# Loading and casting v three pairs later, and issuing the last weight pieces later, in a fused attention and MLP kernel

## The chip, the cores and the metric

The kernel runs on one core of one Trainium2 chip. The metric is the device time of one execution in microseconds (us); lower is better. Engines are named as in the profile: PE is TensorE (matmul), PEld its weight load, DVE is VectorE, ACT is ScalarE, POOL is GpSimd, SP is SyncE, which here issues most of the DMA transfers.

## The reference

There are 8 batches, 12 heads, 448 positions and a head dimension of 64. The inputs are float32, and so is the output.

```python
scores = scale * np.matmul(q, k.transpose(0, 1, 3, 2))
m = np.max(scores, axis=-1, keepdims=True)
e = np.exp(scores - m)
attn = e / (np.sum(e, axis=-1, keepdims=True) + np.exp(-m) + 1e-09)
x = np.matmul(attn, v)              # then (B, H, S, D) -> (3584, 768)

h = x @ w_in                        # 768 x 2048
sp = np.where(h > 20.0, h, np.log1p(np.exp(np.minimum(h, 20.0))))
out = (h * np.tanh(sp)) @ w_out     # 2048 x 768
```

## The kernel before, in words

**Pairs and units.** The work on attention is cut into 48 pairs of heads (6 pairs to a batch). Pairs 0 to 5 form the head of the program, a loop over `p` with four steps `s` each. From pair 6 on, three pairs make a unit `u` (unit 2 is pairs 6 to 8, the third set of three pairs; unit 15 is pairs 45 to 47; units 16 to 19 have no attention left). The loop of a unit has twelve steps `n`, four to each pair.

**One pair.** `load_pair` issues the transfers of q, k and v (224 KB each) on SP into buffers of which there are three for each name. `cast_pair` and `cast_v` turn them into bf16 on POOL (lines 179, 180 and 186). `transpose_pair` (line 206) turns q and k on PE, and `evac_qk` copies them out of PSUM, q as `qd` (line 252 for the later pairs) and k as `kT` (line 260). `scores` (lines 309 to 326) makes the scores on PE and their negative row maximum on DVE (line 330); `exps` takes exponentials on ACT into `en` (line 343). `denominators` and `normalise` follow: from pair 12 on, `normalise` multiplies `en` by the reciprocal on DVE, seven instructions to a pair (line 412); for nearly all pairs a DMA transpose on SP then makes `eT` out of `en` (line 420). `av_pair` multiplies `eT` by v on PE (line 460) and copies the result into `xT`.

**The MLP.** After the twelve steps of a unit come eight groups of six matmuls `x @ w_in` (`mm1_mish`, line 496), each followed by mish on ACT (line 502). The matmuls with `w_out` (`mm2_part`, line 549) are spread over the steps of later units as filler by the table `plan`; the first that read the right half of w_out stand in unit 5.

**Order of the work.** The order on each engine is written out by hand, and each engine, SP and POOL included, works through its queue in that order. In the head, step `s == 3` of pair `p` issues the load of pair `p + 5` and then the DMA transpose of pair `p`, and step `s == 2` casts pair `p + 3`. In a unit, steps 0, 3 and 6 (`LOAD_AT`) load one pair, four ahead of the place (`LEAD`), and cast one pair, three ahead. All three transposes of a unit are issued on SP behind the unit's twelve steps; the next unit's loads are queued behind them.

**The weights.** They come in 20 pieces, in this order: 12 of w_in (256 KB each), 4 of the left half of w_out and 4 of its right half (384 KB each). `load_w` issues them from POOL's queue (line 162). The table `W_AT` says how many go out at which step of units 2, 3 and 4. Where `W_BEHIND` names a pair, POOL first copies a mark out of that pair's `eT` (line 157), so POOL waits until that transpose has landed. Two more places call `load_w` by themselves: two pieces in the head at `p == 1`, and three pieces with a mark on pair 8 behind the fourth matmul group of unit 2.

```python
W_AT = ({0: 4, 5: 1}, {1: 2, 3: 1, 5: 1, 7: 1, 9: 1}, {1: 1, 3: 1, 5: 1, 7: 1})
W_BEHIND = {(0, 0): HEAD - 2, (2, 1): HEAD + 4}
```

`HEAD` is 6. So the marks of the table are on pair 4 (unit 2, step 0) and on pair 10 (unit 4, step 1).

Of the kernel before, what the change touches and what calls it, by code (L numbers as in the profile page):

```python
# [19 lines left out]
def kernel(  # L20
# [27 lines left out]
    N_PAIRS = B * HP  # L48
# [59 lines left out]
    def flush_late():  # L108
        while late:
            late.popleft()()  # L110
# [10 lines left out]
    def load_pair(p, names="qkv"):  # L121
        if p >= N_PAIRS:
            return
        b, h0 = p // HP, (p % HP) * 2
        for nm in names:
            src = dict(q=q, k=k, v=v)[nm]
            t = ld_pool.tile([SP_, 2, NT * D], FP32, tag=f"{nm}_f", name=f"{nm}_f")
            nc.sync.dma_start(
                out=t, in_=src[b, h0 : h0 + 2].rearrange("h (p t) d -> p h (t d)", t=NT)
            )  # L130
            loaded.setdefault(p, {})[nm] = t
# [33 lines left out]
    def cast_pair(p, with_v=True):  # L165
        if p >= N_PAIRS:
            return
        q_f, k_f, v_f = (loaded[p].get(nm) for nm in "qkv")
        q_bf = bf_pool.tile([SP_, NT, 2, D], BF16, tag="q_bf", name="q_bf")
        k_bf = bf_pool.tile([SP_, NT, 2, D], BF16, tag="k_bf", name="k_bf")  # L170
        v_bf = bf_pool.tile([SP_, 2, NT * D], BF16, tag="v_bf", name="v_bf", bufs=12)
        by_t = "p h (t d) -> p t h d"
        q_t, k_t = (t.rearrange(by_t, t=NT) for t in (q_f, k_f))
        if p == 0:
            nc.vector.tensor_copy(out=k_bf, in_=k_t)
            for half in (slice(0, NT // 2), slice(NT // 2, NT)):
                nc.vector.tensor_copy(out=q_bf[:, half], in_=q_t[:, half])
        else:
            nc.gpsimd.tensor_copy(out=q_bf, in_=q_t)  # L179
            nc.gpsimd.tensor_copy(out=k_bf, in_=k_t)  # L180
        casted[p] = (q_bf, k_bf, v_bf)
        if with_v:
            cast_v(p)

    def cast_v(p):
        nc.gpsimd.tensor_copy(out=casted[p][2], in_=loaded.pop(p)["v"])  # L186

    def transpose_pair(p, bank=None):
# [93 lines left out]
    def scores_ahead(limit):  # L282

        while rg["next"] < limit and rg["used"] < len(sc_tiles):
            rg["used"] += 1
            scores(rg["next"])
            rg["next"] += 1
# [301 lines left out]
    LEAD = UNIT_PAIRS + 1  # L589
    LOAD_AT = (0, 3, 6)  # L590
    HEAD = HP
# [2 lines left out]
    AV_AT = {0: {1: 3, 5: 4, 8: 5}, 1: {1: 8, 4: 6, 8: 7}}  # L594
    RDEN_AT = {0: {0: 3, 2: 4, 6: 5}, 1: {0: 8, 2: 6, 6: 7}, 2: {3: 10, 5: 11}}

    W_AT = ({0: 4, 5: 1}, {1: 2, 3: 1, 5: 1, 7: 1, 9: 1}, {1: 1, 3: 1, 5: 1, 7: 1})
    W_BEHIND = {(0, 0): HEAD - 2, (2, 1): HEAD + 4}
    for p, names in (0, "kq"), (1, "qk"), (0, "v"), (2, "qk"), (1, "v"), (2, "v"):
        load_pair(p, names)  # L600
    keep_busy(8, bank=sc_tiles[0][:, 0, :])
    for p in range(2):
        cast_pair(p, with_v=False)
        transpose_pair(p)
        if p == 0:
            evac_qk(p)
            scores_ahead(3)
    load_pair(3)
    cast_v(0)
    cast_pair(2, with_v=False)  # L610
    cast_v(1)
    cast_v(2)
    load_pair(4)


    for p in range(HEAD):
        for s in range(STEPS):
            exps(p * STEPS + s)
            if s == 0 and p == 0:
                evac_qk(1, act=True)  # L620
            flush_late()
            if s == 1:
                late.extend(held)
                held.clear()
                flush_late()
            if s == 2:
                evac_qk(p + 2, act=p % 2 == 0)
            scores_ahead(HEAD * STEPS + 3)
            if s == 0:
                transpose_pair(p + 2)  # L630
                if p:
                    denominators(p - 1)
            if s == 1 and p:
                turn_on_pe(p - 1, NT - 1)
            if s == 3 and p == 1:
                load_w(2)
            if s == 2:
                if p >= 3:
                    spread_rden(p - 3)
                cast_pair(p + 3)  # L640
            if s == 3:
                if p >= 3:
                    av_pair(p - 3, hold=True)
                if p + 5 < 10:
                    load_pair(p + 5)
                normalise(p, dma=p not in BY_PE)
            if s < 3:
                keep_busy(2, half=p)
    denominators(HEAD - 1)

    for u in range(UNITS_PER_B, N_UNITS + 2 * UNITS_PER_B):
        attn = u < N_UNITS
        filler = deque()
        for part in plan.get(u, []):
            filler.extend(mm2_part(*part))
        total, done, acc = sum(w for _, w in filler), 0, 0.0
        p0 = u * UNIT_PAIRS
        if attn and u >= first_mm2:
            av_with.update({p0 + i: p0 + i - UNIT_PAIRS for i in range(UNIT_PAIRS)})
        end = min((u + 1) * UNIT_PAIRS, N_PAIRS) * STEPS  # L660

        for n in range(steps):
            pi, s = divmod(n, STEPS)
            p, idx = p0 + pi, p0 * STEPS + n
            late_tp = u == UNITS_PER_B and n == STEPS
            exps(idx)
            if u == UNITS_PER_B + 1 and n == 0:
                for j in range(2):
                    turn_on_pe(HEAD, j, busy_first=3)
            flush_late()  # L670
            if late_tp:
                transpose_pair(p0 + 2)
                evac_qk(p0 + 2)
            if held and n == 1:
                late.extend(held)
                held.clear()
                flush_late()
            late.extend(slow)
            slow.clear()
            acc += weight[n]  # L680
            want = int(total * acc / sum(weight) + 1e-6)
            while done < want:
                fn, w = filler.popleft()
                fn()
                done += w
            scores_ahead(end)
            if n in LOAD_AT:
                load_pair(p0 + LOAD_AT.index(n) + LEAD)
                cast_pair(p0 + LOAD_AT.index(n) + LEAD - 1)
            for pe, n0 in BY_PE.items():  # L690
                j = n - n0
                first = 2 if pe == HEAD else 0
                if pe // UNIT_PAIRS == u - 1 < first_mm2 - 1 and first <= j < NT:
                    turn_on_pe(pe, j, busy_first=1)
            spread = RDEN_AT.get(u - UNITS_PER_B, {})
            if n in spread:
                on_act = u < first_mm2
                spread_rden(
                    spread[n], copy=nc.scalar.copy if on_act else nc.vector.tensor_copy,
                    behind=slow if on_act else late,  # L700
                )
            early = AV_AT.get(u - UNITS_PER_B)
            if early is not None and n == 7:
                keep_busy(6, bank=mo_free[0])
            if early is not None:
                if n in early:
                    av_pair(early[n], half=p)
            elif s == (2 if pi else 0) and N_PAIRS <= p < N_PAIRS + UNIT_PAIRS:
                av_pair(p - UNIT_PAIRS)
            if u - UNITS_PER_B < len(W_AT):  # L710
                at = (u - UNITS_PER_B, n)
                load_w(W_AT[at[0]].get(n, 0), behind=W_BEHIND.get(at))
        assert done == total

        moe = u < N_UNITS + UNITS_PER_B
        b, w = (u - UNITS_PER_B) // UNITS_PER_B, u % UNITS_PER_B
        nxt = p0 + UNIT_PAIRS
        todo = sorted(range(p0, nxt), key=lambda p: p in BY_PE)
        for f in range(FF_U):
            if moe:  # L720
                mm1_mish(b, w * FF_U + f)
            if u == UNITS_PER_B and f == 3:
                load_w(3, behind=p0 + 2)
            if not attn:
                continue
            if f == 0:
                denominators(p0, UNIT_PAIRS)
                for p in todo if p0 < LATE_DIV else todo[:1]:
                    normalise(p, dma=p not in BY_PE)
            if f == 5 and u == UNITS_PER_B + 1:  # L730
                spread_rden(p0, copy=nc.scalar.copy)
            if f == 4:
                scores_ahead(min(nxt * STEPS + 1, N_PAIRS * STEPS))
            if f in (1, 3, 5):
                transpose_pair(nxt + f // 2, bank=f // 2 % 2)
                evac_qk(nxt + f // 2)
            if f >= FF_U - 2:
                scores_ahead(min(nxt * STEPS + f - FF_U + 4, N_PAIRS * STEPS))
            if f in (3, FF_U - 1) and p0 >= LATE_DIV:
                p = todo[1 + f // (FF_U - 1)]  # L740
                normalise(p, dma=p not in BY_PE)
# [32 lines left out]
```

## Time and profile before

| | |
|---|---|
| median of 3 runs | 483.12 us (481.99 to 483.59) |
| the profiled execution | 483.9 us, span 482.0 us |
| mean granted TensorE clock | 0.992 |
| busy share of PE, DVE, ACT, POOL | 95%, 75%, 72%, 22% |
| moved by DMA | 91.10 MB, 189 GB/s over the span |
| HBM read, written | 45.61 MB, 11.01 MB |
| POOL waiting for marks on `eT` | 27.2 us in 3 waits, the longest 13.8 us |

The profile is of one execution. The span runs from the first to the last instruction; the time of an execution has a little more around it, 1.9 us here. An engine's busy share is a mean over the whole span, in which stages with different limits follow one another. A timeline line gives the start, the length, the engine, the line of the kernel, the operation with what it writes and reads, the number of instructions merged into it, and in brackets the idle time before it and what ended that. For SP the length of a line is the time that the issue took, not the transfer; when a transfer has landed is a time of its own in the trace.

### The profile page before, as it was taken

The numbers are of one execution on the slowest core, as the hardware profiler recorded it, in microseconds if no ns is written. First come the engines' busy times: TensorE is split into PE (matmuls) and PEld (weight loads), VectorE is DVE, ScalarE is ACT, GpSimd is POOL, SyncE is SP. The second block draws the span as 40 slices with busy tenths as digits, with TensorE's granted clock in tenths as the row PEclk, the third lists the DMA queues.
The fourth block names the chain that finished last, engine by engine and source line by source line (L and its number), as shares of the span: only waits on it lengthen the run. The fifth ranks groups of instructions, "written<-read, shape, count | busy, mean of one in ns | idle before, by whom it ended". The sixth has DMA issues, their size and how long they took to land.

```text
span 482.0 us, 9366 instructions
## 1 busy us (share of the span) xinstructions
PE 460.2 (95%) x3291; PEld 257.7 (53%) x3291; DVE 360.3 (75%) x715; ACT 345.3 (72%) x907; POOL 104.3 (22%) x187
## 2 busy tenths in 40 slices
PE   7788899999899999999999999999999999999996
PEld 2344445545555555556555565555555565556563
DVE  5989748669899888889898998888898879421021
ACT  5998868888687869788797968787887978312300
POOL 4633618106022220404040311204040200000000
PEclk9989999999999999999999999999999999999999
DMA  8999999999999979998999999989979695961122
GB/s 238 228 207 220 239 204 216 160 197 248 211 251 228 250 157 211 229 182 224 201 251 164 256 164 219 220 193 227 194 222 197 160 175 121 154 141 34 34 66 67
DMA packets 204976, 91.10 MB, mean 189 GB/s; under 512 B 161792, under 2 KB 201472, under 8 KB 204928
## 3 DMA queue, kind: packets, MB, share of 16 engines
q1 hardware_dynamic: 197408, 84.18, 81.1%
q0 software_dynamic: 7488, 6.29, 9.0%
q8 instruction: 26, 0.43, 0.4%
q14 instruction: 22, 0.18, 0.1%
q10 hardware_dynamic: 32, 0.02, 0.0%
HBM read 45.61 MB, written 11.01 MB: 117 GB/s over the span
## 4 chain that ended last, share of the span: by engine, by line
PE 65%; DVE 7%; ACT 6%; DMA 6%; issue 1%; SPq 0%; DVEq 0%
PE mo L549 23%; PE mo L496 22%; PE sc L309 7%; ACT en L343 6%; PE sc L460 5%; DMA eT<-en 5%; DVE negm L330 4%; PE sc L496 3%; PE sc L206 3%; DVE en L412 1%; DVE xT L473 1%; PE mo L460 1%; DVE o_sb L532 0%; DMA out_dram<-o_sb 0%; DVE qd L252 0%
## 5 line engine op out<-in xcount | busy, mean ns | idle before, releaser
L343 ACT ACTIVATE en<-sc,negm 128x448 bf16<-128x448 f32 x336 | 209.2, 644 | 22.3 <-DVE negm L330 20.6
L330 DVE TENSOR_REDUCE negm<-sc 128x2 f32<-128x896 f32 x192 | 182.8, 970 | 40.6 <-PE sc L309 30.1
L549 PE MATMUL mo<-w_out_sb,gT 128*128 128x384 bf16 (+1 forms) x1024 | 166.7, 306 | 0.4 <-DVE rb L400 0.4
L496 PE MATMUL mo<-xT,w_in_sb 128*128 128x448 bf16 x672 | 142.2, 352 | 1.3 <-DMA w_in_sb<-in_moe_w_in_dram 0.9
L549 PEld LDWEIGHTS <-gT 128*128 128x128 bf16 x1024 | 96.3, 98 | 56.0 <-issue 1.9
L502 ACT ACTIVATE gT<-mo 128x448 bf16<-128x448 f32 x112 | 59.5, 543 | 81.1 <-PE mo L496 80.9
L496 PEld LDWEIGHTS <-w_in_sb 128*128 128x128 bf16 x768 | 72.5, 98 | 65.0 <-issue 3.2
L412 DVE TENSOR_SCALAR en<-en,rden 128x448 bf16<-128x448 bf16 x252 | 74.7, 369 | 0.8
L179 POOL CAST q_bf<-q_f 112x512 bf16<-112x512 f32 x47 | 29.2, 622 | 211.7 <-DMA q_f<-in_q_dram 191.2
L309 PE MATMUL sc<-kT,qd 128*128 128x448 bf16 x252 | 71.6, 354 | 1.8 <-DVE qd L252 1.8
L343 ACT ACTIVATION_READ_ACCUMULATOR en<-sc,negm 128x1 f32 x336 | 72.1, 215 | 0.0
L532 DVE COPY o_sb<-mo 128x384 f32<-128x384 f32 (+1 forms) x64 | 31.9, 498 | 48.3 <-PE mo L549 48.1
L460 PE MATMUL sc<-eT,v_bf 112*64 112x448 bf16 x336 | 39.8, 357 | 1.7 <-DMA eT<-en 0.9
L309 PEld LDWEIGHTS <-qd 128*128 128x128 bf16 x252 | 24.5, 98 | 30.7 <-issue 12.9
L252 DVE TENSOR_SCALAR qd<-sc 64x448 bf16<-64x448 bf16 x72 | 27.8, 386 | 6.0 <-PE sc L206 5.2
L186 POOL CAST v_bf<-v_f 112x512 bf16<-112x512 f32 x48 | 30.0, 625 | 5.7 <-DMA v_f<-in_v_dram 5.4
L180 POOL CAST k_bf<-k_f 112x512 bf16<-112x512 f32 x47 | 29.3, 624 | 7.2 <-DMA k_f<-in_k_dram 5.9
L460 PEld LDWEIGHTS <-v_bf 112*64 112x64 bf16 x384 | 19.8, 109 | 20.5 <-issue 11.8
L260 ACT COPY kT<-sc 128x448 bf16<-128x448 bf16 x39 | 20.8, 533 | 0.6 <-PE sc L206 0.6
L496 PE MATMUL sc<-xT,w_in_sb 128*128 128x448 bf16 x96 | 20.8, 352 | 0.0
L473 DVE CAST xT<-sc 128x448 bf16<-128x448 f32 x33 | 20.3, 615 | 0.0
L206 PEld LDWEIGHTS <-q_bf 112*128 112x128 bf16 x192 | 13.5, 97 | 9.2 <-issue 1.0
(61 smaller groups left out, 281.2 us busy)
## 6 DMA issues: line engine op xcount, KB each, us to landing
k_f<-in_k_dram SPq DMA_DIRECT2D x48, 224.0 KB, 5.0
q_f<-in_q_dram SPq DMA_DIRECT2D x48, 224.0 KB, 4.8
v_f<-in_v_dram SPq DMA_DIRECT2D x48, 224.0 KB, 5.2
w_in_sb<-in_moe_w_in_dram POOLq DMA_DIRECT2D x12, 256.0 KB, 9.5
w_out_sb<-in_moe_w_out_dram POOLq DMA_DIRECT2D x8, 384.0 KB, 10.4
out_dram<-o_sb SPq DMA_DIRECT2D x7, 336.0 KB, 4.0
out_dram<-o_sb SPq DMA_DIRECT2D x8, 288.0 KB, 4.6
out_dram<-o_sb SPq DMA_DIRECT2D x8, 240.0 KB, 3.2
```

Source lines behind the costliest of these rows:

```text
L179: nc.gpsimd.tensor_copy(out=q_bf, in_=q_t)
L180: nc.gpsimd.tensor_copy(out=k_bf, in_=k_t)
L186: nc.gpsimd.tensor_copy(out=casted[p][2], in_=loaded.pop(p)["v"])
L309: nc.tensor.matmul(sc[:, bk, 0:S], lhsT=qT[:, i].rearrange("d h r -> d (h r)"), rhs=kT, start=True, stop=True,)
L330: half_max[p] = nc.vector.tensor_reduce(out=negm, in_=sc[:, 0 : len(cols), 0:S], axis=AX.X, op=ALU.max, negate=True)
L343: e = nc.scalar.activation(out=st["en"][:, :, c, 0:SP_], in_=sc[:, bk, 0:S].rearrange("q (j c) -> q j c", j=NT), func=AF.Exp, bias=st["neg ...
L412: nc.vector.tensor_scalar(out=en[:, :, i, 0:SP_], in0=en[:, :, i, 0:SP_], scalar1=st["rden"][:, i : i + 1], scalar2=None, op0=ALU.mult,)
L460: mm = nc.tensor.matmul(av[h * 64 : (h + 1) * 64, 0:S], lhsT=v_bf[:, h, j * D : (j + 1) * D], rhs=e_h, start=(j == 0), stop=(j == NT - 1),)
L496: nc.tensor.matmul(h_ps[:, 0:S], lhsT=w_in_sb[:, dm, ff * 128 : (ff + 1) * 128], rhs=xT[b][:, dm, :], start=(dm == 0), stop=(dm == DM_T - 1),)
L502: nc.scalar.activation(out=gT[:, ff, b % 2 * S : b % 2 * S + S], in_=h_ps[:, 0:S], func=AF.Mish)
L532: nc.vector.tensor_copy(out=o_sb[:, cols.start : cols.start + n_dve], in_=st["o"][:, 0:n_dve])
L549: nc.tensor.matmul(st["o"][:, 0:n_cols], lhsT=gT[:, ff, i * 128 : (i + 1) * 128], rhs=w_out_sb[:, ff, cols], start=(ff == 0), stop=(ff == ...
```

## The change

In the head, pairs 0 to 6 are loaded with their v as before, and pairs 7, 8 and 9 without it; v of pairs 6, 7 and 8 is not cast there. In the units, steps 0, 3 and 6 still load q and k four pairs ahead and cast q and k three ahead, but the v that they load is one pair ahead and the v that they cast is the pair of the place itself. So unit 2 loads v of pairs 7, 8 and 9 and casts v of 6, 7 and 8, and the last v's are loaded and cast in unit 15.

Of the weights, the last four pieces (the right half of w_out) are issued in unit 4 at steps 3 (one), 5 (one) and 7 (two) where it was one each at steps 1, 3, 5 and 7. The casts of pair 16 stand ahead of them at step 3. The mark on pair 10 is left out.

```diff
     def cast_v(p):
+        if p >= N_PAIRS:
+            return
         nc.gpsimd.tensor_copy(out=casted[p][2], in_=loaded.pop(p)["v"])
...
-    W_AT = ({0: 4, 5: 1}, {1: 2, 3: 1, 5: 1, 7: 1, 9: 1}, {1: 1, 3: 1, 5: 1, 7: 1})
-    W_BEHIND = {(0, 0): HEAD - 2, (2, 1): HEAD + 4}
+    W_AT = ({0: 4, 5: 1}, {1: 2, 3: 1, 5: 1, 7: 1, 9: 1}, {3: 1, 5: 1, 7: 2})
+    W_BEHIND = {(0, 0): HEAD - 2}
...
             if s == 2:
                 if p >= 3:
                     spread_rden(p - 3)
-                cast_pair(p + 3)
+                cast_pair(p + 3, with_v=p + 3 < HEAD)
             if s == 3:
                 if p >= 3:
                     av_pair(p - 3, hold=True)
                 if p + 5 < 10:
-                    load_pair(p + 5)
+                    load_pair(p + 5, "qkv" if p + 5 <= HEAD else "qk")
                 normalise(p, dma=p not in BY_PE)
...
             if n in LOAD_AT:
-                load_pair(p0 + LOAD_AT.index(n) + LEAD)
-                cast_pair(p0 + LOAD_AT.index(n) + LEAD - 1)
+                at = p0 + LOAD_AT.index(n)
+                load_pair(at + LEAD, "qk")
+                load_pair(at + 1, "v")
+                cast_pair(at + LEAD - 1, with_v=False)
+                cast_v(at)
```

## The prediction

> **What bounds the kernel now.** I read the page first, then the chain of waits in order of time, then the timelines of PE, SP, POOL and DVE up to 125 us, and the trace's landing time of each transfer. The page:
>
> ```profile
> PE 460.2 (95%) x3291; PEld 257.7 (53%) x3291; DVE 360.3 (75%) x715; ACT 345.3 (72%) x907; POOL 104.3 (22%) x187
> ...
> PE 65%; DVE 7%; ACT 6%; DMA 6%; issue 1%; SPq 0%; DVEq 0%
> ```
>
> PE is busy for 460.2 of 482.0 us. Its idle time before single instructions, where it is over 0.15 us, adds up to 16.2 us, and all but 0.28 us of that lies before 122.1 us: from there on PE runs without a gap, so an edit can win only what it takes out of the first quarter (or lose what it adds anywhere). The DMA part of the chain is one transfer, and behind it stands a DVE step:
>
> ```profile
> 76.17 25.10 DMA eT<-en
> ...
> 101.31 0.95 PE sc L460 x8
> ...
> 116.31 2.93 DVE en L412 x5
> 119.23 1.48 issue
> 120.72 0.57 DVE en L412 x2
> ...
> 122.05 0.55 PE sc L309 x2
> ```
>
> A transpose has a median of 6.7 us from issue to landing (page, part 6); the one of pair 9, issued at 76.17, needed 25.10. PE's timeline gives the three late stalls that I work with:
>
> ```profile
> 58.48 1.69 PE L496 MATMUL mo<-xT,w_in_sb 128*128 128x448 bf16 x8 [0.92 <-DMA w_in_sb<-in_moe_w_in_dram]
> ...
> 101.31 0.95 PE L460 MATMUL sc<-eT,v_bf 112*64 112x448 bf16 x8 [0.86 <-DMA eT<-en]
> ...
> 122.05 0.55 PE L309 MATMUL sc<-kT,qd 128*128 128x448 bf16 x2 [1.75 <-DVE qd L252]
> ```
>
> Counted from matmul start to matmul start, the first is 1.08 us (58.485 - 57.216 - 0.189), with 0.28 us more at 64.10, on the piece that landed at 64.06; the second about 1.0 us. What comes before them is SP's queue in the head:
>
> ```profile
> 30.03 0.41 SPq L128 DMA_DIRECT2D v_f<-in_v_dram  x1
> 30.53 4.47 SPq L420 DMA_TRANSPOSE eT<-en  x1
> 35.10 0.53 SPq L128 DMA_DIRECT2D q_f<-in_q_dram  x1
> ...
> 43.02 0.41 SPq L128 DMA_DIRECT2D v_f<-in_v_dram  x1
> 43.53 3.93 SPq L420 DMA_TRANSPOSE eT<-en  x1
> 47.55 0.53 SPq L128 DMA_DIRECT2D q_f<-in_q_dram  x1
> ```
>
> SP runs back to back from 28.9 to 54.3 us. The transpose of pair 4 starts at 43.53, though ACT ended that pair's exponentials at 34.9: SP is 8.7 us late. POOL's mark on that transpose ends its wait at 50.14, right after the landing at 50.09, and only then do four w_in pieces go out:
>
> ```profile
> 50.14 0.18 POOL L157 COPY marks<-eT 1x2 bf16<-1x2 bf16 x1 [2.66 <-DMA eT<-en]
> 50.27 2.88 POOL L162 DMA_DIRECT2D w_in_sb<-in_moe_w_in_dram  x4
> ...
> 104.35 0.18 POOL L157 COPY marks<-eT 1x2 bf16<-1x2 bf16 x1 [13.78 <-DMA eT<-en]
> 104.58 0.79 POOL L162 DMA_DIRECT2D w_out_sb<-in_moe_w_out_dram  x1
> 112.49 0.61 POOL L179 CAST q_bf<-q_f 112x512 bf16<-112x512 f32 x1 [7.12 <-DMA q_f<-in_q_dram]
> ```
>
> The first of those four landed at 58.44, which ends the first stall. So loads, transpose, mark and pieces are one chain that PE waits for.
>
> **The change, part by part.** *The head loses three v loads* (pairs 7, 8, 9), three of 224 KB. From unit 2 on each slot again issues q, k and one v, and casts q, k and one v; only the v's pair is three lower. So later slots are unchanged in instructions and bytes, unit 15 gets two loads and three casts that it did not have, and the buffers come free at the same places (v of pair 9 waits for the cast of pair 6, which now stands where the cast of pair 9 stood).
>
> What a load is worth: on SP it is 0.50 us (30.03 to 30.53); in the full queue neighbouring loads land 0.7 to 0.85 us apart (32.37, 33.19, 33.89). So the transpose of pair 4 lands earlier by 1.5 (3 x 0.5, SP's time alone) to 2.4 us (3 x 0.8). I take 2.0, nearer the spacing, since SP's transposes stretch with the traffic ahead of them (3.93 to 9.26 us in the head) and the DMA engines are full (share 1.06 to 1.10 of 16 engines from 28 to 50 us). The q and k of pair 9, cast ahead of the mark, move with it. The three v casts taken out of the head (0.62 us each) were hidden in POOL's waits: nothing.
>
> *Term A, the w_in stalls.* Four pieces land 2.0 us earlier: 56.4 against PE's need at 57.4, and 62.1 against 62.8 (64.1 less 1.35). Both stalls go: 1.08 + 0.28, say 1.3; if only 1.5 us arrive, still 1.3, and 0.9 if ACT, which loads its mish table until 59.63, frees the first PSUM bank too late for the third or fourth group. The PE gain carries through, since ACT's exponentials of unit 3 (71.16) stand behind the last mish, which stands behind PE.
>
> *Term B, the transpose of pair 9.* It starts when pair 9's exponentials end, now 1.3 us earlier, but lands when the traffic before and beside it is done (the fourth w_out piece lands at 98.51, the transpose at 101.27), and all that is released by the transpose of pair 8 and its mark at 70.39, which move by the 2.0. PE arrives 1.3 earlier, the transpose 2.0: 0.7 of the 1.0 us goes (bounds 0.15 for a shift of 1.5, 1.0 for 2.4).
>
> *Term C, the last four w_out pieces.* The mark on pair 10 (13.78 us of POOL waiting) goes, but the cast behind it then waits for q of pair 16, whose load SP issues only at 106.62, after its three transposes: the wait stays, with another name. The first piece, at 104.58 before, now goes out behind the casts of 16 and so no longer takes DMA time from the nine loads at 106.6 to 112.7, which landed 5.7 to 8.3 us after issue against 3.4 to 5.0 one unit later (136 to 143 us). So I expect q of pair 16 some 4 us earlier, 107.6 to 108.5, and POOL's burst of nine casts and four piece issues to end near 116 to 117 instead of 120.67. That matters to DVE:
>
> ```profile
> 116.31 4.99 DVE L412 TENSOR_SCALAR en<-en,rden 128x448 bf16<-128x448 bf16 x7
> ...
> 122.84 1.81 DVE L412 TENSOR_SCALAR en<-en,rden 128x448 bf16<-128x448 bf16 x7
> ```
>
> The same seven instructions take 1.81 us alone and 4.99 beside POOL's casts; one of them, of a median 331 ns, took 1,864 beside three casts in a row. They stand ahead of the qd copies that PE waits 1.75 us for. With A and B they start at 114.3 and overlap POOL for some 2 us instead of 4.4: half of the 3.2 us of slowing stays, and of the stall 0.5. Gain 1.2 (bounds 1.75, and minus 0.75 if the burst does not move, since it then holds one more piece issue).
>
> The Trainium skill ("SBUF — State Buffer", Who interferes with whom) says that VectorE in a two-port mode and GpSimd hold their shared port pair for a whole instruction and the other blocks fully. The trace agrees: 1,864 ns is three casts of 0.62. By that rule C goes in steps of one cast between its bounds, and the sum lies anywhere from 1.3 to 3.8.
>
> *Later.* The late v loads and casts cost nothing: v of pair 15 is cast around 117 to 121 us and first used at 156.85; in unit 15 SP is idle between 405.2 and 411.2 and POOL has nothing. Without that slack two loads would cost 1.0 us of SP.
>
> Sum: 1.3 + 0.7 + 1.2 = 3.2 us. The profiled execution took 483.9 us (span 482.0); it would take 480.7. The median of the three runs is 483.12, so 479.9. A measurement can tell about 0.3% (1.45 us) from no change.
>
> **The rivals.** *C fails*: the burst moves no more than PE does, A and B stand: 2.0 us, 481.1. For it: SP's loads and PE move nearly together. Against: the piece at 104.58 is gone from their way. Chance 0.13.
>
> *The head's lead is given back*: the transposes take as long as the engines need for them, whatever stands ahead (the trace has stretches of 155 and 122 GB/s around 36 and 40 us), and the pieces come under 1 us earlier; only part of A is left, 0 to 1.3 us, about 482.4. Against: a load is bytes of its own, 0.7 to 0.85 us apart in landing. Chance 0.20.
>
> *Slower: the bunched pieces starve the transpose of pair 12.* In the trace, pair 9's transpose met four w_out pieces and moved at 49 GB/s beside their 142 (packets of 92 to 94 us). Now again four pieces go out together. The transpose of pair 12 is issued at 121.35, landed at 128.63 with the last piece landing at 125.30, and PE wants it at 130.36: a margin of 1.7 us, and 2.3 and 1.5 for the two behind it. One more piece is 1.8 us at some 215 GB/s. It decides once the last piece lands after 127.1 on this clock; with no lead from the head and a second 1.8 us lost to sharing, PE stalls about 2 us: 485.1, and at the price of pair 9 much more. Against: with the lead the last piece lands near 121 to 123. Chance 0.17. The Trainium skill ("DMA: Bandwidth & Descriptors", Queues, rings and completion order) says that each DMA engine takes the queues in turn, a packet at a time; that speaks against this change in the same way, and the slowed transpose agrees with it.
>
> **How the numbers follow.** Forecast 0.50, at 479.9; with C failing 0.13, both faster by over 0.3%: 0.63. Lead given back: same, 0.20. Slower: 0.17. The bounds of the three terms (gains of 4.05 and 0.3) give 479.1 to 482.8; 0.7 below for PE's small gaps at 106.71 (0.33) and 110.80 (0.37), and 0.4 for the spread of the runs. The range 478.0 to 484.3 takes in the forecast, both weak cases and the near part of the slower one. The likeliest cases alone: 478.0 to 481.5.
>
> **What would show it.** Right: no PE wait on w_in; pair 4's transpose landing near 48; the mark at 70.39 near 68.4; pair 9's transpose not waited for, or under 0.4 us; the first seven L412 of unit 4 in about 3.4 us; PE's score matmul of pair 15 (122.05) at about 118.9. Wrong: w_in waits as before (A), the burst on POOL still covering the seven (C), or a wait of PE on eT between 125 and 140 us, which would be the slower rival.

## The result, and the profile after

The change makes the kernel faster: a median of 480.07 us in 7 runs against 482.39 us for the kernel before in 7 runs beside it, ratio 0.9942 with a 95% interval of 0.9921 to 0.9962. By the ratio that is 2.8 us (1.8 to 3.8); the medians alone are 2.3 us apart. In a second set of runs the ratio was 0.9950 (0.9927 to 0.9972). The forecast was 479.9 us, 3.2 us less than the 483.12 us that stood for the kernel before when it was made. The profiled execution took 479.66 us, span 477.9.

On the page after, the DMA part of the chain of work that ended last, 6% before, is gone.

```profile
PE 69%; DVE 8%; ACT 6%; issue 1%; DVEq 0%
```

SP's timeline in the head shows why. Line numbers after are two higher than before from `cast_v` on (L420 is now L422).

```profile
28.81 0.53 SPq L128 DMA_DIRECT2D q_f<-in_q_dram  x1
29.44 0.41 SPq L128 DMA_DIRECT2D k_f<-in_k_dram  x1
29.94 4.03 SPq L422 DMA_TRANSPOSE eT<-en  x1
...
40.59 0.41 SPq L128 DMA_DIRECT2D k_f<-in_k_dram  x1
41.11 4.02 SPq L422 DMA_TRANSPOSE eT<-en  x1
45.22 0.53 SPq L128 DMA_DIRECT2D q_f<-in_q_dram  x1
```

SP starts this stretch at the same time as before (28.81, before 28.90), but the transpose of pair 4 goes out at 41.11 instead of 43.53: 2.4 us gained over three pairs, 0.8 for each load that is gone. It landed at 47.00 (50.09 before, 49.48 in a second profile of before). POOL's timeline follows it:

```profile
47.05 0.17 POOL L157 COPY marks<-eT 1x2 bf16<-1x2 bf16 x1 [0.96 <-DMA eT<-en]
47.18 2.90 POOL L162 DMA_DIRECT2D w_in_sb<-in_moe_w_in_dram  x4
...
107.49 0.61 POOL L179 CAST q_bf<-q_f 112x512 bf16<-112x512 f32 x1 [18.66 <-DMA q_f<-in_q_dram]
...
115.89 0.64 POOL L188 CAST v_bf<-v_f 112x512 bf16<-112x512 f32 x1
```

The four w_in pieces go out 3.1 us earlier, q of pair 16 is cast 5.0 us earlier, and POOL's burst ends at 116.5 instead of 120.67. The wait in front of that cast is indeed the old one with another name: 18.66 us for the load, where 13.78 us stood for the mark and 7.12 for the load. The lines of PE that answer to the three stalls:

```profile
56.31 2.44 PE L498 MATMUL mo<-xT,w_in_sb 128*128 128x448 bf16 x12
...
99.35 0.95 PE L462 MATMUL sc<-eT,v_bf 112*64 112x448 bf16 x8 [0.62 <-ACT en L345]
...
118.40 0.55 PE L311 MATMUL sc<-kT,qd 128*128 128x448 bf16 x2
```

The twelve w_in matmuls now run on without a break. At the product of pair 9 (99.35) a wait of 0.62 us remains, but it ends with an exponential on ACT, not with the transpose (landed at 96.67). The score of pair 15 has no wait. DVE, ahead of it:

```profile
113.91 3.73 DVE L414 TENSOR_SCALAR en<-en,rden 128x448 bf16<-128x448 bf16 x7
...
119.20 1.81 DVE L414 TENSOR_SCALAR en<-en,rden 128x448 bf16<-128x448 bf16 x7
```

Seven instructions take 3.73 us instead of 4.99; the prediction said about 3.4. The slowing is thus only in part gone, and yet PE does not wait.

### The profile page after: what moved, and what is told of

The parts are those of the page before. It is cut to its first block, busy times and chain, and to the rows that moved or that the text cites. A ratio compares the mean times of both kernels' runs of the same rounds, so it can differ in the third digit from the quotient of the medians.

```text
span 477.9 us, 9363 instructions
## 1 busy us (share of the span) xinstructions
PE 458.8 (96%) x3291; PEld 257.8 (54%) x3291; DVE 358.7 (75%) x715; ACT 344.7 (72%) x907; POOL 103.8 (22%) x186
## 4 chain that ended last, share of the span: by engine, by line
PE 69%; DVE 8%; ACT 6%; issue 1%; DVEq 0%
PE mo L498 24%; PE mo L551 24%; PE sc L311 7%; ACT en L345 6%; PE sc L462 6%; DVE negm L332 5%; PE sc L498 3%; PE sc L208 3%; DVE en L414 1%; DVE xT L475 1%; PE mo L462 1%; DVE o_sb L534 1%; PE mo L272 0%; DVE eT L437 0%; ACT L345 0%
## 5 line engine op out<-in xcount | busy, mean ns | idle before, releaser
L414 DVE TENSOR_SCALAR en<-en,rden 128x448 bf16<-128x448 bf16 x252 | 74.2, 367 | 0.8
L345 ACT ACTIVATION_READ_ACCUMULATOR en<-sc,negm 128x1 f32 x336 | 71.0, 211 | 0.0
```

Of the source, the lines that this page charges most:

```text
L345: e = nc.scalar.activation(out=st["en"][:, :, c, 0:SP_], in_=sc[:, bk, 0:S].rearrange("q (j c) -> q j c", j=NT), func=AF.Exp, bias=st["neg ...
L414: nc.vector.tensor_scalar(out=en[:, :, i, 0:SP_], in0=en[:, :, i, 0:SP_], scalar1=st["rden"][:, i : i + 1], scalar2=None, op0=ALU.mult,)
```

## The experiments

Between single executions even an unchanged kernel differs, so I measured PE's progress by stretches, from the starts of its matmuls in each trace: A, from the first to the 48th w_in matmul of unit 2; B, from the first w_in matmul of unit 3 to the product of pair 9; C, from the 25th w_in matmul of unit 4 to the first of unit 5; and the end, from the end of the last matmul to the end of the span. All in us.

| kernel (profile) | A | B | C | end |
|---|---|---|---|---|
| before | 12.27 | 15.55 | 22.95 | 4.66 |
| before, again | 11.25 | 15.31 | 22.38 | 4.67 |
| after | 10.90 | 15.30 | 21.27 | 4.19 |
| after, again | 10.93 | 15.30 | 21.03 | 4.17 |
| weight part alone | 11.65 | 15.30 | 21.25 | 4.20 |
| v part alone | 10.90 | 15.30 | 21.55 | 4.35 |
| v part alone, again | 10.90 | 15.30 | 21.03 | 4.35 |
| v one pair later | 11.16 | 15.30 | 22.32 | 4.19 |
| before, casts of 18 held | 11.45 | 15.31 | 21.19 | 4.66 |
| before, casts of 18 held, again | 10.97 | 15.31 | 22.11 | 4.66 |
| v part, casts of 18 held | 10.90 | 15.30 | 21.15 | 4.35 |
| early piece | 10.90 | 16.76 | 21.02 | 4.19 |
| late pieces | 10.90 | 15.30 | 25.17 | 4.18 |

The stretches between these agree in all of them: 16.85 us from A to B's start, 17.7 from B to C, 314.2 to 314.4 from unit 5 to the last w_in matmul. What comes before A does not: its first matmul starts between 55.6 and 57.4 us, with no order by kernel (after 56.31 and 55.64, before 56.64 and 56.51). Single profiles are compared by stretches for that reason.

**The kernel before, again**, unchanged.

> The kernel before, unchanged, for a second profile of it. My theory: ratio 1.000 within 0.2%; the three stalls of the first profile come again at the same places, the two DMA waits within 0.3 us; the stall ahead of pair 15's first score may differ by up to one cast (0.6 us), since it hangs on which instruction comes first. Rival (the first profile's stall was an accident of that execution): the 1.75 us stall is under 0.5 us.

Ratio 0.9998 (0.9975 to 1.0021). Of the three stalls, the 0.92 us on w_in is not there in this execution (the first piece landed at 56.66, in time; 0.18 us on a later piece is), the product of pair 9 waits for ACT, and 0.88 us of the last one stays:

```profile
99.93 0.95 PE L460 MATMUL sc<-eT,v_bf 112*64 112x448 bf16 x8 [0.62 <-ACT en L343]
...
119.79 0.55 PE L309 MATMUL sc<-kT,qd 128*128 128x448 bf16 x2 [0.88 <-DVE qd L252]
```

So my own expectation that the two DMA waits come back within 0.3 us failed: they are races that some executions lose and others win. And behind the wait on the transpose lies one on ACT of 0.62 us, which stands in every profile in which the transpose of pair 9 is in time.

**The weight part alone.** The kernel before with

```diff
-    W_AT = ({0: 4, 5: 1}, {1: 2, 3: 1, 5: 1, 7: 1, 9: 1}, {1: 1, 3: 1, 5: 1, 7: 1})
-    W_BEHIND = {(0, 0): HEAD - 2, (2, 1): HEAD + 4}
+    W_AT = ({0: 4, 5: 1}, {1: 2, 3: 1, 5: 1, 7: 1, 9: 1}, {3: 1, 5: 1, 7: 2})
+    W_BEHIND = {(0, 0): HEAD - 2}
```

> The kernel before with only the weight part of the change (pieces at steps 3, 5 and 7 of unit 4, no mark on pair 10). My theory (v part gives terms A and B, weight part gives term C): the waits on w_in stay (0.92 us at 58.5) and the wait on the transpose of pair 9 stays (0.86 us); q of pair 16 lands some 2 us sooner, POOL's burst ends near 118.5 instead of 120.7, and the 1.75 us stall ahead of pair 15's first score falls to 0.3 to 0.8. About 1.2 us faster than before, 481.2. Rival (the mark held everything, and the whole gain is the weight part): as fast as the full change, 2.3 to 2.8 us faster than before.

Ratio 0.9968 (0.9948 to 0.9989), 1.5 us faster. A wait of 0.50 us on w_in stays (A is 11.65), and the stall ahead of pair 15's score is gone (C 21.25); 0.3 to 0.8 us of it was expected to stay. The wait on pair 9's transpose, which was expected to stay too, is not there (B 15.30). The rival with the whole gain in this part falls by its profile: the weight part does not mend A.

**The v part alone.** The kernel after with the two lines above turned back.

> The kernel after with the weight pieces and the mark on pair 10 as before: only the v part of the change. My theory: no wait on w_in, transposes of pairs 4 and 9 land 2 to 4 us earlier, PE reaches the product of pair 9 about 2.0 us earlier; the burst moves with it, so most of the 1.75 us stall stays. 2.0 us faster than before, 480.4. Rival (whole gain is the weight part): 0 to 0.5 us. Rival (the v part carries all): 2.8 us or more.

Ratio 0.9941 (0.9918 to 0.9963), as fast as the whole change. A is 10.90, and C, which I had put down to the weight part, falls to 21.55 too. I had expected POOL's burst of casts to move no more than PE does. It moved further: it ended 2.7 us behind the start of the seven instructions on DVE, and 1.7 us in the second run below, where both profiles of before have 4.4 us; the seven took 3.30 and 2.83 us. A second run:

> The v part alone a second time, beside the two others. The first time it was 0.9941 of before (0.9918 to 0.9963), as fast as the full change. If the weight part adds its own gain to it (my first theory: terms A and B from v, C from the weights), this run is 0.5 us or more slower than the kernel after's 0.9942 and 0.9950, about 0.996. If the v part alone carries the whole gain, 0.994 to 0.995 again.

Ratio 0.9968 (0.9956 to 0.9980); A 10.90, C 21.03. This is the time expected if the weight part adds its own gain, and the first run has the one expected if it does not. The v part alone is worth 1.5 to 2.9 us, and whether the weight part adds to it (0 to about 1 us) is not settled by these times. The stretches say that it can add little: the two parts remove the same stall in C, and only the v part removes A.

**The casts beside VectorE.** In the kernel before, ahead of unit 5's first step:

```diff
+            if u == UNITS_PER_B + 3 and n == 0:
+                load_w(0, behind=p0 - UNIT_PAIRS)
             exps(idx)
```

> The kernel before with one mark more: at the start of unit 5, ahead of the casts of pair 18, POOL waits until the transpose of pair 12 has landed (about 128.6 us). Nothing else changes. If the casts beside VectorE make the seven L412 slow (my theory for term C), the last four of the seven run at 0.33 us, the seven take 3.0 us instead of 4.99, the stall ahead of pair 15's first score falls from 1.75 to under 0.4, and the kernel is 1.3 to 1.7 us faster than before: about 481. Rival (the seven are slowed by something else, such as the traffic of the weight pieces): no change, 482.4.

The casts of pair 18 are out of the way here, and those of pair 17 ended at 115.85, just behind the start of the seven. The seven take 1.94 us, though the weight pieces are still in flight (the last landed at 123.35). So it is POOL's work beside them that slows them, and not the traffic:

```profile
115.70 1.94 DVE L412 TENSOR_SCALAR en<-en,rden 128x448 bf16<-128x448 bf16 x7
117.56 1.60 DVE L252 TENSOR_SCALAR qd<-sc 64x448 bf16<-64x448 bf16 x4
```

C is 21.19, as after. But the time fell only to 0.9991 (0.9972 to 1.0010). So I ran it again.

> The kernel before with the casts of pair 18 held behind the transpose of pair 12, a second time. Its first profile showed the seven L412 in 1.94 us and no stall, as term C says, but the time fell by 0.4 us only (interval from 1.35 faster to 0.5 slower). If the gain of the removed stall is real and the first figure was low by chance: ratio 0.997 to 0.998, seven L412 under 2.2 us, and 21.2 us again between the 25th matmul group's start of unit 4's MLP and the first w_in matmul of unit 5 (22.4 and 23.0 in the two profiles of before). If the hold brings a cost of its own: ratio 0.999 or more again, and a stall of PE or a late load behind 125 us in this profile.

Ratio 0.9998 (0.9982 to 1.0014). The seven take 1.94 us again, and C is 22.11 all the same: here the gain is given back at the product of pair 13.

```profile
127.66 0.95 PE L460 MATMUL sc<-eT,v_bf 112*64 112x448 bf16 x8
...
133.68 0.95 PE L460 MATMUL sc<-eT,v_bf 112*64 112x448 bf16 x8 [1.04 <-DVE negm L330]
```

The profile names a DVE reduction, but in the first run of this kernel the same product started while that reduction was still running. What is common is the landing of pair 13's transpose: 133.55 here, 0.13 us ahead of the product, and 0.13 to 0.14 us ahead of it also in the first run, in the second profile of before, with v one pair later and with the late pieces. In the first profile of before, PE was 2.26 us behind that landing, since it had stood 1.75 us before. Take that stall away, and the transpose of pair 13 is next. This shows one way in which the gain is lost; that the first run's times show no gain although its C is 21.19 stays unexplained.

**Both.** The v part alone with the same hold:

> The v part alone (weight pieces and the mark on pair 10 as before) with the casts of pair 18 held behind the transpose of pair 12: the head's relief of the change, and the other way to part the casts from VectorE. If the v part leaves a stall of 0.34 us in that place and the hold takes it away: 0.2 to 0.4 us faster than the kernel after, ratio to before 0.993 to 0.994. If the hold has a cost of its own: 0.995 or more.

Ratio 0.9965 (0.9953 to 0.9977), beside 0.9968 of the v part alone in the same runs. With the head relieved, the transpose of pair 13 lands 2.64 us ahead of its product, so nothing is given back, but there is also nothing left in C to win (21.15). The further 0.2 to 0.4 us that I had thought possible did not come.

**One load instead of three.** The kernel after with v one pair later than before:

```diff
-                cast_pair(p + 3, with_v=p + 3 < HEAD)
+                cast_pair(p + 3, with_v=p + 3 < HEAD + 2)
-                    load_pair(p + 5, "qkv" if p + 5 <= HEAD else "qk")
+                    load_pair(p + 5, "qkv" if p + 5 <= HEAD + 2 else "qk")
-                load_pair(at + 1, "v")
+                load_pair(at + 3, "v")
-                cast_v(at)
+                cast_v(at + 2)
```

> The kernel after with v one pair later than before instead of three: only v of pair 9 leaves the head, weight part as in the kernel after. If each load taken out of the head moves the transpose of pair 4 by its own share (my theory), it lands near 48.8 us (49.5 and 50.1 in the two profiles of before, 47.0 after), the second to fifth w_in piece follow it, and the time lies between the weight part alone (0.9968 of before) and the full change (0.9942): about 0.996, 480.9. Rival (the loads taken out matter only together, through SP's buffers or a late slot): the landing stays at 49.5 or later and the time is that of the weight part alone.

Ratio 0.9982 (0.9966 to 0.9998). The transpose of pair 4 landed at 49.66; counted back from PE's first w_in matmul, 7.4 us ahead of it, where the kernels with the old head have 6.5 to 7.5 and those with three loads less 8.6 to 11.3. One load hardly shows, so the price of a load is not a fixed amount. A is 11.16, and C has a stall of 1.00 us at the product of pair 13, whose transpose landed 0.14 us before. The time lies behind the full change, as my theory has it, but not between it and the weight part alone (0.9968): by its ratio it is slower than both. On the landing, the rival's number came.

**An earlier piece.** The kernel after with the first of the four at step 1, without a mark:

```diff
-{3: 1, 5: 1, 7: 2})
+{1: 1, 3: 1, 5: 1, 7: 1})
```

> The kernel after with the first of the last four w_out pieces at step 1 of unit 4 again, but without the mark on pair 10: POOL issues it at about 88.8 us, behind the casts of pair 15, while the transpose of pair 9 is under way. My theory (a weight piece beside a transpose takes most of the rate): that transpose lands 1.8 to 2.7 us later than after (96.7), at 98.5 to 99.4, where PE wants it at 98.7: a wait of 0 to 0.7 us, partly given back by a shorter burst. 480.1 to 480.8. Rival (the transpose is not touched by one piece): lands at 96.7, and the kernel is as fast as after or up to 0.4 us faster.

Ratio 0.9977 (0.9957 to 0.9997), about 1.5 us slower than after. One piece, issued at 89.84 beside the transpose of pair 9, delayed its landing to 101.81. That is 44.5 us behind PE's first w_in matmul, where the kernel after has 40.4: 4.1 us later. B grew by 1.46 us:

```profile
101.86 0.95 PE L462 MATMUL sc<-eT,v_bf 112*64 112x448 bf16 x8 [2.08 <-DMA eT<-en]
```

I had expected 0 to 0.7 us. The old mark on pair 10 was thus no waste: it kept the piece away from this transpose. The casts of pair 16 keep it away as well, since they wait for a load that is queued behind the transposes.

**Late pieces.** This brings about the slower rival of the prediction. The kernel after without the table's pieces of unit 4; behind the first matmul group of that unit, POOL waits for the reciprocals and then issues them:

```diff
+                if u == UNITS_PER_B + 2:
+                    nc.gpsimd.tensor_copy(out=marks[0:1, 3, 0:2], in_=att[p0]["rden"][0:1, 0:2])
+                    load_w(4)
```

> The kernel after with the last four w_out pieces held until the reciprocals of unit 4 are there (a mark on them behind the first matmul group): the four go out at 114.3 to 117.3 us, in the way of the transpose of pair 12, issued near 117. This brings about the slower rival of the prediction. If pieces starve a transpose (as that rival says), the last piece lands at 125 to 127, pair 12's transpose at 128 to 130 instead of 125.4, and PE, which wants it at 126.7, waits 1.5 to 3 us: 482 to 483, no faster than before. Otherwise: landing within 1 us of 125.4, no wait, 480.

Ratio 1.0020 (1.0005 to 1.0036), slower than before. The pieces went out at 115.1 to 118.1, the last landed at 127.60 and the transpose of pair 12 at 130.48; two products wait for transposes:

```profile
130.52 0.95 PE L462 MATMUL sc<-eT,v_bf 112*64 112x448 bf16 x8 [1.95 <-DMA eT<-en]
136.44 0.76 PE L462 MATMUL sc<-eT,v_bf 112*64 112x448 bf16 x6 [0.94 <-DMA eT<-en]
```

The stall of 0.96 us ahead of pair 15's score, which I had not expected here, is back as well. The seven instructions on DVE are slow again, though POOL's casts meet only their end:

```profile
114.81 4.62 DVE L414 TENSOR_SCALAR en<-en,rden 128x448 bf16<-128x448 bf16 x7
...
115.08 3.01 POOL L162 DMA_DIRECT2D w_out_sb<-in_moe_w_out_dram  x4
118.05 0.65 POOL L179 CAST q_bf<-q_f 112x512 bf16<-112x512 f32 x1
```

One of the seven took 2.21 us, from 116.63 on, and 1.42 us of that lies before the first cast, while POOL was issuing the pieces. So POOL's issues of pieces, and not its casts alone, seem to slow DVE; no run here has the issues without the casts behind them.

**The kernel after, again**, unchanged.

> The kernel after, unchanged, in the same runs as these three, for its spread and a second profile. The two profiles of before differ by 1.8 us, in the three stalls of the prediction: w_in 0.92 and none, transpose of pair 9 0.86 and none, pair 15's score 1.75 and 0.88. If the change removes stalls that come in some executions only, the second profile of after has none of the three and lies within 0.7 us of the first, and the spread of the runs is about half of that of before (4.4 us). Rival (the change is a shift, with the same chance events on top): a spread like before's, and a stall over 0.5 us in the second profile.

Ratio 0.9950 (0.9927 to 0.9972). The second profile has none of the three stalls, and A, B and C agree with the first within 0.25 us, where the two profiles of before differ by 1.0, 0.2 and 0.6. The expectation that the runs spread half as widely is not borne out: their standard deviation is 1.07 us in 11 runs, that of before beside them 1.03 us in 34 (in the first runs it was 0.39 against 0.79, in 7 each). What spreads less is stretch A (10.97 to 12.27 in the five profiles with the old head, 10.90 to 10.93 in the seven with three loads less); for the time as a whole it is not shown.

## Why the prediction was right

**The chain in the head** held, link by link: SP's queue, the transpose of pair 4, the mark, the pieces, PE. The size was too small: the transpose landed 3.1 us earlier, for 2.0 forecast and an upper bound of 2.4 (also 3.1 between the means of the five profiles with the old head and the seven with three loads less). Three times the spacing of two loads was not the right measure, since one load less moved nothing.

**Term A** was the right mechanism and too large. Forecast 1.3 us; the two profiles of before stand 1.37 and 0.35 above the 10.90 of every kernel with the relieved head (mean 0.9; 0.6 over the five profiles of kernels with the old head, which range from 0.1 to 1.4). The mis-sized step is the price: I took the stall of one execution as that of all.

**Term B** was nearly nothing: 0.25 and 0.01 us in place of 0.7. The step that failed is "about 1.0 us" for the wait on pair 9's transpose: a wait on ACT of 0.62 us stands at the same matmul and stays when the transpose is early. A wait was priced without asking what is late next.

**Term C** came out larger, 1.5 us (22.95 and 22.38 against 21.27 and 21.03) for 1.2 forecast, and that POOL's work is behind it is shown by the held casts; that a shared port is the way was not measured. The step that was mis-sized is "of the stall 0.5" that was to stay: the seven still took 3.73 us, and nothing of the stall stayed. I was also wrong on whose gain it is: the prediction gave it to the weight part, yet the v part alone removes the stall too. Whether the gain lasts hangs on pair 13's transpose. With three loads less in the head it landed 0.3 to 2.7 us ahead of its product in six of seven profiles (late pieces is the seventh). With the old head or one load less it landed 0.13 to 0.17 us ahead, and PE waited up to 1.0 us for it; only in the first profile of before was it early, because PE was late. The weight part alone, at 0.17 us, got by without a wait. What carries the relief in the head on to 130 us is not shown.

**The sum**: 0.9 + 0.1 + 1.5 = 2.5 us of PE, and 0.5 us at the end of the program, which I had not forecast (4.66 against 4.18, in the drains after the last store; it goes with both parts, 4.35 with v and 4.20 with the weights, and I have no cause for it). That makes 3.0, a little above the measured 2.3 to 2.8 and below the forecast 3.2. The agreement is in part luck: an A and a B that were 1.0 us too large together were made up by C and by an end of the program that nobody foresaw. That the forecast time, 479.9, is 0.2 us from the measured 480.07 is luck as well: it was counted from a median of three runs, 483.12, which lies 0.7 us above that of seven.

**The rivals.** "C fails" and "the lead is given back" did not come. The slower rival's mechanism is real and near: with the pieces 2.5 to 4.1 us later, counted from PE's first w_in matmul, C is 3.9 us longer (0.96 of that is a stall on DVE, whose L414 met POOL's issues and casts), and in the kernel after pair 13's transpose lands only 0.3 to 0.5 us ahead of its product.

## What to carry to other kernels

When an in-order queue is late on what matters, count what could leave it without being missed soon: three loads whose v PE read 43 us or more after they had landed held up a transpose, a mark behind it and weight pieces that PE waited for. Price a stall by what would be late next at the same instruction, and by more than one execution: races on a full DMA queue come and go. And the gain of a stall removed in one place lasts only if the next transfer is early enough; in the profiles with three loads less it was, the late pieces apart.

## What the runs showed of the hardware

Two things were larger than I had expected. POOL's work slowed a DVE step of 1.81 us to 4.99, 4.54 and 3.73 by where the casts fell. Where no cast met the step (the second profile of after) it took 1.81 us, and 1.94 where only the last 0.15 us of one did, with weight pieces in flight both times. The casts are not all of it: in late pieces the step took 4.62 us, more than half of its delay beside POOL's issues of pieces and ahead of the first cast, and in the first profile of after the first of the seven took 1.56 us, 0.79 of it before the first cast. A single issue cost little: one instruction of 0.46 us instead of 0.33 in both held kernels.

And one 384 KB piece on POOL's own DMA queue, in flight for 9.9 us beside a transpose on SP's queue, put off that landing by 4.1 us; at the 215 GB/s that the prediction worked with, its bytes are 1.8 us. How uneven the sharing is can be read from the packets of the first profile of before: between 92 and 94 us the pieces' queue moved 370 packets of 768 bytes, and SP's queue 379 of 256 bytes, nearly as many packets and a third of the bytes. The Trainium skill ("DMA: Bandwidth & Descriptors", Queues, rings and completion order) says that the queues are served in turn, by packets. The nearly equal counts agree with that, if the profile's packets are the ones meant there, which no run here shows. Beside the single piece of the early-piece kernel the sharing was less uneven: 426 packets of 768 bytes against 889 of 256 between 95 and 99 us.
